# Six y pairs in the key sweep instead of four, and 35 instead of 32 steps of the second MLP product as seven products

## The chip, the core and the metric

The kernel runs on one core of one Trainium2 chip. A core has five engines that work from queues of their own: TensorE (PE in the profile, with its weight loads as PEld), VectorE (DVE), ScalarE (ACT), GpSimd (POOL) and SyncE (SP, which here only issues transfers). The metric is the device time of one execution in microseconds; the median of several is compared.

## The reference

For x of 2048 tokens with 576 features, a gate mixes a linear attention block and a channel MLP of width 4608:

```python
x = A_x
g = _sigmoid((x * gate_w).sum(-1, keepdims=True))
# a: 32 heads of 18; phi(t) = where(t > 0, t + 1, exp(t)) + 1e-6
pq, pk = phi(q), phi(k)
kv = jnp.einsum("bhsd,bhse->bhde", pk, v)
z = jnp.einsum("bhsd->bhd", pk)
o = num / den            # num = pq kv, den = pq z + 1e-6
a = o @ wo
y = _layernorm(x, axis=-1)
h = _gelu(jnp.einsum("bsd,df->bsf", y, w1) + b1)
b = jnp.einsum("bsf,fd->bsd", h, w2) + b2
return g * a + (1 - g) * b
```

## The kernel before

Every float32 operand of a large product is split into a high half, rounded to TensorE's fast float32 form (by a copy on ACT), and a low half, the rest (by a subtraction on DVE). Three products of halves replace one.

**The key sweep** goes over 16 tiles of 128 tokens, in the order `ORDER`. In each tile n TensorE projects the keys in two halves (into PSUM banks 6 and 7), adds the first part of the previous tile's products of keys and x, projects the queries in two halves (banks 6 and 7 again) and adds the rest of those products. The last three tiles leave their queries to later, so their tiles are shorter; the late queries of the first of these three follow right behind tile 15. A bank is free again when the projection in it has been through phi: Relu and Exp on ACT, then one DVE instruction that writes the keys (`k`) or the queries (`acc`). DVE and ACT also split the next tile's x, the keys (`ks`) and the tile's rows for the products (`xs`).

**Gates.** For groups of tiles (`MOMENTS`) the mean, the deviation and the gate are worked out: `gates_in` (three small DVE instructions), one step later `gates_act` (Exp, a table load, Sqrt, a table load, a dummy Exp, all on ACT), one step later `gates_out` (eight small DVE instructions) and `share_moments` (a store by POOL's queue, from which `rows` is read back over all partitions).

**Y pairs.** The normalized x, transposed, is the MLP's moving operand. It is made for two tiles at a time, a pair: the raw rows and the two tiles' x are loaded into `yr` and `rows` (both within the tile `accs`), normalized in four DVE instructions of 768 columns (`normal_pair`), combined in four DVE sums of 384 (`sum_pair`) and split in seven matrices: three double parts and a single one, each a copy on ACT and two instructions on DVE into a stage (`ys` in the profile, `y` for the last part), then stored. Part 0 needs only the normalizing, part 1 the first two sums, parts 2 and 3 the others. There are eight pairs, four for each half of the tokens.

The sweep's own work is written in order; beside it stand jobs at thirds of a tile: `run(3 * n)` behind the split of the keys, `run(3 * n + 1)` behind the queries' phi, `run(3 * n + 2)` at the tile's end. `Y_JOBS` names for each pair the third in which it is loaded, and those of its normalizing, sums and parts. The first half's four pairs are made in the sweep; the second half's four in the first half of the feed-forward part (`make_y`), one matrix at a time through `ystage`.

**The MLP** runs in 36 steps, 18 for each half of the tokens. A step's first product (up, `product`, in seven products by Strassen's scheme in Winograd's form) fills two blocks of 256 hidden features; ACT's Gelu and splits on ACT and DVE make h; the second product (down) is `one_of_seven` where the step stands in `SEVEN` (14 units of 6 matmuls of 128x288, 84 in all) and `plain_unit` where it does not (8 units of 12, 96 in all). Seven products need four sums of h, four sums of w2, seven low halves of h instead of four and four groups of w2 instead of two. `FIVES` names the steps of seven that keep one of the products in a sum of its own, with fewer evictions on DVE. `ON_DVE` tells for each sum of h, w1 and w2 whether DVE or POOL makes it. Up matmuls stream 512 columns, down matmuls 288.

The order of the feed-forward part on all engines is set by a planner, `plan`, from costs, due times and the table `TUNED`; TensorE takes the next up or the next down piece by `choose`. What the planner chose is issued in that order on each engine and stays so: every instruction is recorded through `InOrder`, so an engine never passes a waiting instruction. All instructions show the recorder's line, L120.

Of the kernel before, what the change touches and what calls it, by code (L numbers as in the profile page):

```python
# [33 lines left out]
MOMENTS = ((0, 2), (2, 4), (4, 6), (6, 8), (8, 16))  # L34
# [42 lines left out]
Y_JOBS = ((13, (16, 16, 17, 17), (18, 18, 19, 19), (18, 19, 20, 21)), (20, (22, 22, 23, 23), (25, 25, 27, 27), (25, 26, 28, 29)), (27, (31, 31, 32, 32), (33, 33, 34, 34), (34, 35, 35, 36)), (35, (37, 37, 38, 38), (39, 39, 41, 41), (40, 42, 43, 44)))  # L77
# [6 lines left out]
SEVEN = set([1, 2, 3, 4, 5, 7, 8, 9, 10, 11, 12, 14, 15, 16, 17, 18, 19, 20, 21, 22, 23, 24, 25, 26, 27, 28, 29, 30, 31, 32, 33, 34])  # L84
DVE_SUMS = set([(2, False), (2, True), (3, True), (4, False), (4, True), (6, False), (6, True)])
SEEDS = ((0, 0, 0), (0, 1, 1), (1, 0, 1))
Y_EARLY = 5000
ON_DVE = set([('h', 0, 2), ('h', 0, 6), ('h', 1, 3), ('h', 2, 2), ('h', 2, 6), ('h', 3, 4), ('h', 3, 6), ('h', 4, 2), ('h', 5, 3), ('h', 5, 6), ('h', 6, 2), ('h', 6, 3), ('h', 6, 6), ('h', 7, 2), ('h', 7, 6), ('h', 8, 4), ('h', 8, 6), ('h', 9, 4), ('h', 9, 6), ('h', 10, 2), ('h', 10, 4), ('h', 11, 2), ('h', 11, 6), ('h', 12, 4), ('h', 12, 6), ('h', 13, 4), ('h', 14, 4), ('h', 14, 6), ('h', 15, 2), ('h', 15, 4), ('h', 16, 6), ('h', 17, 3), ('h', 17, 4), ('w1', 2, 0), ('w1', 3, 0), ('w1', 10, 0), ('w1', 12, 0), ('w1', 14, 0), ('w1', 16, 0), ('w1', 17, 0), ('w2', 0, 0), ('w2', 4, 0), ('w2', 5, 0), ('w2', 8, 0), ('w2', 10, 0), ('w2', 11, 0), ('w2', 12, 0), ('w2', 14, 0), ('w2', 16, 0)])
FIVES = set([1, 2, 3, 4, 5, 7, 8, 9, 10, 11, 12, 14, 15, 16])
TUNED = (6, 7, 0, 1000, 0, {'unit': -1500, 'ytl': 1500, 'h': -1500, 'yst': 700, 'yhi': -300, 'y': -1500, 'w2': -3000, 'sum': 700, 'p': 700, 'ylo': 300, 'w1sum': -700, 'w1raw': 1500, 'evict': -1500, 'w2hi': -700, 'fin': -700, 'q2': -1500, 'seed': -3000, 'hi': -3000, 'ynorm': 3000, 'forked': -1500, 'ysum': -1500, 'q4': 6000, 'whole': 700, 'u3': -700, 'b2b': -3000, 'q1': 10000, 'out': -300, 'u1': -300, 'end': -700, 'q3': 700, 'w1st': 3000, 'attn': -700, 'fold': -300, 'w2raw': 300, 'yraw': 700}, [2, 5, 250, -500, 600, {'sum': 700, 'u3': 700, 'end': -1500, 'w2sum': -700, 'out': -3000, 'unit': -1500, 'p': -700, 'h': -300, 'evict': -700, 'hi': -1500, 'w1sum': 10000, 'seed': 3000, 'forked': 3000, 'y': 3000, 'q2': -3000, 'u1': -1500, 'q4': 6000, 'w1st': 300, 'ysum': 300, 'w2': 300, 'yraw': 1500, 'whole': 300, 'ynorm': 10000, 'attn': -3000, 'ytl': -1500, 'w1raw': -300, 'q1': 1500, 'yst': 300, 'fin': -300, 'yhi': 700, 'w2raw': 1500, 'w1': 300, 'w2hi': 6000, 'fold': 10000, 'b2b': 700}])  # L90
# [36 lines left out]
def tile_gated_mix(ctx: ExitStack, tc: tile.TileContext, x, xm, xe, wm, we, wvm, wve, wo, um, ue, w2, b1, b2, gw, out):  # L127
# [278 lines left out]
    def load_pair(sup, j):  # L406
# [3 lines left out]
        sp.dma_start(rows, moments[b][None, :, c0:c0 + 2 * P].to_broadcast([P, 2, 2 * P]))  # L410
        for a, m in enumerate((B11, B12)):
            i = ORDER[q + a]
# [147 lines left out]
    jobs = {n: [] for n in range(3 * NT)}  # L560
# [15 lines left out]
    for b, n in enumerate((9, 13, 22, 28)):  # L576
# [4 lines left out]

    for j, (loaded, normal, added, parts) in enumerate(Y_JOBS):
        at(loaded, load_pair, 0, j)
        for n, when in enumerate(normal):
            at(when, normal_pair, 0, j, n // 2, n % 2)
        for m, when in enumerate(added):
            at(when, sum_pair, 0, j, m)
        for part, when in enumerate(parts):
            at(when, split_pair, 0, j, part, lambda part=part: y_stages[part])
            at(when, split_tails, 0, j, part)  # L590
            at(when + 2, store_pair, 0, j, part)
# [290 lines left out]
    HEAR = {PE: 155, ACT: 33, DVE: 33, POOL: 78, DMA: 30}  # L882
# [141 lines left out]
    def sum_on(what, k, m=0):  # L1024
        own = ((what, k, m) in ON_DVE) != ((m, k < NCHUNK) in DVE_SUMS)
# [26 lines left out]
    def make_w1(k):  # L1052
# [5 lines left out]
        if k > 1:  # L1058
            dma(lambda: load_w1(k), raw_free["w1"] if k > 2 else [], [("w1raw", k)], 4400, 8, each=560)
            for n in range(4):  # L1060
                engine, eng = sum_on("w1", k)
# [33 lines left out]
    def make_w2(k):  # L1095
# [4 lines left out]
        if seven:  # L1100
            for n in range(4):
                engine, eng = sum_on("w2", k)
# [317 lines left out]
    def plan(lag, late, slop, slack, guard, ahead, second=None):  # L1420
        second = second or (lag, late, slop, slack, guard, ahead)
# [23 lines left out]
        next_up, next_down, shift = 0, 0, 0.0  # L1445
# [35 lines left out]
        def choose(e, gently):  # L1481
            if e == PE:
# [4 lines left out]
                if a and b:  # L1487
# [5 lines left out]
                    if ta is not None and tb is not None:  # L1493
                        if tb <= ta + 100:
# [22 lines left out]
        while any(pending.values()):  # L1517
# [6 lines left out]
            e, t = o.engine, s + o.tail  # L1524
# [92 lines left out]
```

## Time and profile before

| | |
|---|---|
| median of 3 runs | 1096.38 us (1096.2 to 1096.6) |
| span of the profiled execution, first to last instruction | 1094.1 us |
| the runs' median over this span | 2.3 us |
| sweep of the keys, first tile with its full rhythm to the key sums | 26 to 181 us |
| a tile with queries, a tile without | 11.2 us, 7.5 us |
| linear attention | to 272.6 us |
| feed-forward part, up and down matmuls | 272.6 to 1090.5 us |

The profile is of one execution. Its views are read in this manner: the page gives busy time of each engine over the whole; the view by stretches gives the same for chosen windows; the timeline lists instructions with start, length and, in brackets, the idle time before them and what ended it. A matmul's end is modelled, and they overlap, so the spacing is read from start to start.

### The profile page before, as it was taken

To read this page: it belongs to the slowest core of one execution; us is meant where nothing else is said; L and a number is where in the kernel's file an instruction comes from. 1 tells how busy PE (TensorE), PEld (TensorE's weight loads), DVE (VectorE), ACT (ScalarE), POOL (GpSimd) and SP (SyncE) were. 2 spreads that over 40 slices of the span, in tenths; PEclk is the share of its full clock that TensorE was granted. 3 is DMA by queue.
4 is the path that set the end of the run, shared out by engine and by line. 5 is a ranking of instruction groups with operands and counts; after the bars stand their busy time and mean duration, and the time that the engine had idled before them with its cause. 6 is when DMAs were issued, how large, how long until landed. Compare 5 with 4: busy or idle time off the path is not lost.

```text
span 1094.1 us, 18599 instructions
## 1 busy us (share of the span) xinstructions
PE 1087.8 (99%) x6694; PEld 996.8 (91%) x6694; DVE 917.2 (84%) x1553; ACT 687.5 (63%) x1230; POOL 235.6 (22%) x232
## 2 busy tenths in 40 slices
PE   9999999999999999999999999999999999999998
PEld 9999999999898889988889999989899999999898
DVE  4568784895799999899999997988887888878888
ACT  6677765454667887777877876455545555455552
POOL 2111112531123232332111202121122211221110
PEclk9999999999999999999999999999999999999999
DMA  6466772745745565764556559574444435444432
GB/s 186 128 88 190 171 218 102 286 173 188 252 152 195 184 206 192 235 215 161 199 174 222 195 192 395 174 253 119 138 145 118 130 119 150 132 119 119 135 100 87
DMA packets 109006, 189.72 MB, mean 173 GB/s; under 512 B 8940, under 2 KB 68604, under 8 KB 104818
## 3 DMA queue, kind: packets, MB, share of 16 engines
q1 hardware_dynamic: 108002, 187.78, 53.3%
q8 instruction: 53, 0.87, 0.3%
q10 hardware_dynamic: 720, 0.74, 0.2%
q14 instruction: 39, 0.32, 0.1%
q0 software_dynamic: 192, 0.01, 0.1%
HBM read 121.70 MB, written 66.80 MB: 172 GB/s over the span
## 4 chain that ended last, share of the span: by engine, by line
PE 93%; DVE 3%; DMA 1%; ACT 1%; issue 0%; SPq 0%; ACTq 0%; DVEq 0%
PE ps L120 93%; DVE accs L120 1%; DMA s<-in_wm 0%; DVE h L120 0%; DMA fresh<-in_ue 0%; DMA ystage<-late_acc 0%; ACT u L120 0%; DMA s<-in_we 0%; DVE wp L120 0%; DVE region L120 0%; SPq L120 0%; DVE den L120 0%; DVE fresh L120 0%; DVE ystage L120 0%; DVE u L120 0%
## 5 line engine op out<-in xcount | busy, mean ns | idle before, releaser
L120 PEld LDWEIGHTS ps<-region,h 128*128 128x128 f32 x3072 | 437.8, 188 | 30.1 <-ACT ps L120 4.3
L120 PE MATMUL ps<-region,h 128*128 128x288 f32 x3072 | 457.1, 296 | 1.0 <-DVE region L120 0.4
L120 DVE TENSOR_TENSOR accs<-ps,accs 128x576 f32<-128x576 f32 x330 | 246.1, 753 | 60.9 <-PE ps L120 54.1
L120 PE MATMUL ps<-y,wa 128*128 128x512 f32 x1008 | 257.6, 393 | 0.0
L120 PEld LDWEIGHTS ps<-y,wa 128*128 128x128 f32 x1008 | 180.9, 188 | 30.3 <-ACT ps L120 0.2
L120 POOL TENSOR_TENSOR fresh<-fresh 128x288 f32<-128x288 f32 (+1 forms) x128 | 116.4, 913 | 410.5 <-DMA fresh<-in_w 129.6
L120 PE MATMUL ps<-y,wb 128*128 128x512 f32 x756 | 199.3, 394 | 0.1
L120 DVE TENSOR_TENSOR h<-u,h 128x512 fp32r<-128x512 f32 x240 | 165.9, 704 | 8.7 <-ACT u L120 8.7
L120 PEld LDWEIGHTS ps<-y,wb 128*128 128x128 f32 x756 | 133.9, 188 | 20.9 <-ACT u L120 0.5
L120 ACT ACTIVATE region<-fresh 128x576 fp32r<-128x576 f32 (+1 forms) x132 | 81.3, 625 | 73.5 <-PE ps L120 72.9
L120 PE MATMUL ps<-y 128*128 128x288 f32 (+1 forms) x896 | 125.8, 297 | 0.3 <-DVE y L120 0.2
L120 PEld LDWEIGHTS ps<-y 128*128 128x128 f32 x896 | 122.6, 189 | 1.8 <-DVE y L120 0.4
L120 ACT ACTIVATE ps<-ps 128x576 f32<-128x576 f32 (+1 forms) x127 | 78.7, 621 | 45.0 <-PE ps L120 21.5
L120 POOL TENSOR_TENSOR u<-u 128x512 f32<-128x512 f32 x44 | 57.0, 1296 | 193.5 <-DVE h L120 54.9
L120 DVE TENSOR_TENSOR region<-fresh,region 128x576 fp32r<-128x576 f32 (+1 forms) x132 | 93.8, 723 | 1.1 <-ACT region L120 1.1
L120 ACT ACTIVATE u<-ps 128x512 f32<-128x512 f32 x73 | 43.0, 589 | 68.4 <-PE ps L120 68.2
L120 ACT ACTIVATE h<-u 128x512 fp32r<-128x512 f32 x128 | 73.5, 622 | 10.0 <-DVE u L120 5.5
L120 ACT ACTIVATE h<-u,b1s 128x512 fp32r<-128x512 f32 x73 | 52.6, 722 | 42.6 <-DVE u L120 42.4
L120 PE MATMUL ps<-wp,qt 128*128 128x288 f32 x448 | 63.0, 297 | 0.0
L120 DVE TENSOR_TENSOR u<-ps,u 128x512 f32<-128x512 f32 x74 | 50.4, 683 | 13.5 <-PE ps L120 12.7
L120 PEld LDWEIGHTS ps<-wp,qt 128*128 128x128 f32 x448 | 59.8, 188 | 0.0
L120 DVE TENSOR_TENSOR u<-u 128x512 f32<-128x512 f32 x84 | 58.1, 691 | 1.7 <-POOL u L120 1.1
(137 smaller groups left out, 1052.1 us busy)
## 6 DMA issues: line engine op xcount, KB each, us to landing
w1d<-wa SPq DMA_DIRECT2D x17, 1280.0 KB
wa<-w1d SPq DMA_DIRECT2D x68, 320.0 KB
fresh<-in_w SPq DMA_DIRECT2D x70, 288.0 KB
y<-yd SPq DMA_DIRECT2D x14, 1280.0 KB
w1d<-wb SPq DMA_DIRECT2D x17, 960.0 KB
wb<-w1d SPq DMA_DIRECT2D x51, 320.0 KB
yd<-ystage SPq DMA_DIRECT2D x28, 320.0 KB
fresh<-in_um SPq DMA_DIRECT2D x64, 128.0 KB
```

What stands on the lines that cost most here:

```text
L120: self.last = self.tc.keep_in_program_order(op(*args, **kwargs))
```

## The change

Six pairs are made in the sweep: the first half's four and two of the second half's, one every six thirds of a tile (first parts at 18, 24, 30, 36, 42 and 47). The sixth pair's last parts and their stores stand behind the late queries' projection (48) and behind the last tile's squares (49, 50), for which the list of jobs is three longer. The gates of these tiles are needed earlier, so `MOMENTS` has two more groups of two tiles; their jobs start at `GATES_AT`. `load_pair` is cut in two, and the rows are loaded six thirds after the gates' start at the earliest. `make_y` makes the last two pairs only.

Steps 0, 6 and 13 are added to `SEVEN`; `FIVES` gains 6 and 13 and loses 16. `ON_DVE` now names every sum that DVE makes, for w1 and w2 one by one. The planner gets longer hearing times, a measured cost for each matmul of a run of one kind, and a rule that stays with up matmuls until a run has `hold` of them while the down side is less than `wait` behind; `TUNED` has new numbers.

```diff
-MOMENTS = ((0, 2), (2, 4), (4, 6), (6, 8), (8, 16))
+MOMENTS = ((0, 2), (2, 4), (4, 6), (6, 8), (8, 10), (10, 12), (12, 16))
-Y_JOBS = ((13, (16, 16, 17, 17), (18, 18, 19, 19), (18, 19, 20, 21)), (20, (22, 22, 23, 23), (25, 25, 27, 27), (25, 26, 28, 29)), (27, (31, 31, 32, 32), (33, 33, 34, 34), (34, 35, 35, 36)), (35, (37, 37, 38, 38), (39, 39, 41, 41), (40, 42, 43, 44)))
+Y_JOBS = ((13, (16, 16, 17, 17), (18, 18, 19, 19), (18, 19, 20, 21)), (19, (22, 22, 23, 23), (24, 24, 25, 25), (24, 25, 26, 27)), (25, (28, 28, 29, 29), (30, 30, 31, 31), (30, 31, 32, 33)), (31, (34, 34, 35, 35), (36, 36, 37, 37), (36, 37, 38, 39)), (37, (40, 40, 41, 41), (42, 42, 43, 43), (42, 43, 44, 45)), (43, (45, 45, 46, 46), (47, 47, 48, 48), (47, 48, 48, 49)))
+GATES_AT = (9, 13, 19, 25, 31, 37)
-SEVEN = set([1, 2, 3, 4, 5, 7, 8, 9, 10, 11, 12, 14, 15, 16, 17, 18, 19, 20, 21, 22, 23, 24, 25, 26, 27, 28, 29, 30, 31, 32, 33, 34])
+SEVEN = set([0, 1, 2, 3, 4, 5, 6, 7, 8, 9, 10, 11, 12, 13, 14, 15, 16, 17, 18, 19, 20, 21, 22, 23, 24, 25, 26, 27, 28, 29, 30, 31, 32, 33, 34])
-    for b, n in enumerate((9, 13, 22, 28)):
+    for b, n in enumerate(GATES_AT):
...
+    for pair, (loaded, *_) in enumerate(Y_JOBS):
+        at(max(loaded, GATES_AT[pair] + 6), load_rows, *divmod(pair, TPB))
+        at(loaded, load_xs, *divmod(pair, TPB))
...
     projected(late[0], QUERY)
+    run(3 * NT)
     queries_out(late[0])
     moments_of(end)
+    run(3 * NT + 1)
     for part in range(2):
         add_products(end, part)
+    run(3 * NT + 2)
...
-        for j in range(TPB):
+        for j in range(len(Y_JOBS) - TPB, TPB):
...
-                        if tb <= ta + 100:
+                        if tb <= ta + 100 and not (run[0] == "up" and run[1] < hold and behind < wait and ta <= free[PE]):
```

What stands on ACT from the queries' phi of tile 12 to the keys' phi of tile 13, before (`e` is phi's Relu and Exp; `ys` are double parts of a y pair):

```order
L120 ACTIVATE xs<-xn 128x576
L120 ACTIVATE e<-ps 128x288
L120 ACTIVATE e<-e 128x288
L120 ACTIVATE e<-ps 128x288
L120 ACTIVATE e<-e 128x288
L120 ACTIVATE ys_560<-accs 128x2x384
L120 ACTIVATE ys_561<-accs 128x2x384
L120 ACTIVATE ys_562<-accs 128x2x384
L120 ACTIVATE e<-ps 128x288
L120 ACTIVATE e<-e 128x288
```

And in the change, from the second half of the queries on:

```order
L121 ACTIVATE e<-ps 128x288
L121 ACTIVATE e<-e 128x288
L121 ACTIVATE ys_565<-accs 128x2x384
L121 ACTIVATE g<-g 128x2
L121 ACT_TABLE_LOAD
L121 ACTIVATE mr_115<-mt 128x2
L121 ACT_TABLE_LOAD
L121 ACTIVATE tiny<-ones 128x1
L121 ACTIVATE ys_566<-accs 128x2x384
L121 ACTIVATE e<-ps 128x288
L121 ACTIVATE e<-e 128x288
```

The first part has moved ahead of the queries, and a gate job stands between the second and the third. Tiles 6, 8 and 10 have the same order in the change.

On DVE, from the keys of tile 15 to the copies of the sums out of PSUM, before (`y<-accs` is the last part of a pair; `acc` are the late queries, for which bank 6 and 7 wait):

```order
L120 SCALAR_TENSOR_TENSOR k<-ps,e 128x288 x2
L120 SCALAR_TENSOR_TENSOR ks<-k,ks 128x576
L120 TENSOR_TENSOR xs<-xn,xs 128x512
L120 TENSOR_TENSOR xs<-xn,xs 128x64
L120 SCALAR_TENSOR_TENSOR acc_102<-ps,e 128x288 x2
L120 COPY accs<-ps 128x512
```

And in the change, behind the same split of tile 15's rows:

```order
L121 TENSOR_TENSOR xs<-xn,xs 128x64
L121 TENSOR_TENSOR y<-accs,y 128x256
L121 SCALAR_TENSOR_TENSOR y<-y,low_rows,accs 128x128
L121 TENSOR_TENSOR accs<-accs 128x768 x4
L121 TENSOR_TENSOR accs<-accs 128x384 x2
L121 TENSOR_TENSOR ys_564<-accs,ys_564 128x2x256
L121 SCALAR_TENSOR_TENSOR ys_564<-ys_564,low_rows,accs 128x2x128
L121 TENSOR_TENSOR accs<-accs 128x384 x2
L121 TENSOR_TENSOR ys_565<-accs,ys_565 128x2x256
```

Behind these come the rest of parts 1 and 2, then the late queries. The fifth pair's last part and the whole sixth pair but its last part have come to stand ahead of them.

On TensorE the feed-forward part has 3036 down matmuls instead of 3072, and 282 runs of up matmuls between down matmuls instead of 298; the up matmuls are 1764 in both.

More of the change, by code (lines that the diff above doesn't have):

```diff
@@ L1024, in sum_on @@
     def sum_on(what, k, m=0):
[L1025 removed]
+        own = (what, k, m) in ON_DVE
         return (DVE, dve) if own else (POOL, pool)
@@ L1418, in tile_gated_mix, with plan @@
     assert len(in_order) == len(ops)
-    def plan(lag, late, slop, slack, guard, ahead, second=None):
-        second = second or (lag, late, slop, slack, guard, ahead)
+    def plan(lag, late, slop, slack, guard, ahead, second, hold, wait):
         slot, due = {o: n for n, o in enumerate(ups)}, {}
@@ L1530, in plan @@
                         late, slop, slack, guard = second[1:5]
+                        hold, wait = second[6:8]
                 else:
```

55 lines of the change are left out of this document (34 added, 21 removed).

## The prediction

> **What bounds the kernel now.** First the page: busy shares, then the chain that ended last.
>
> ```profile
> PE 1087.8 (99%) x6694; PEld 996.8 (91%) x6694; DVE 917.2 (84%) x1553; ACT 687.5 (63%) x1230; POOL 235.6 (22%) x232
> PE 93%; DVE 3%; DMA 1%; ACT 1%; issue 0%; SPq 0%; ACTq 0%; DVEq 0%
> ```
>
> TensorE sets the time: 1087.8 of 1094.1 us busy, 93% of the chain. A matmul that goes is worth its full spacing, and a wait put in front of a matmul costs its full length. So I ask of every stage how near the second engine, VectorE (DVE), stands to TensorE. The view by stretches tells: seven tiles of the key sweep with queries, the three without and what follows them, the first half of the feed-forward part, the second.
>
> ```profile
> 70.80:149.20 78.40, 78.40 (x527) 75.33 (x526) 63.08 (x137) 56.97 (x128) 12.36 (x10) 1.00 0.67 162
> 149.20:181.90 32.70, 32.70 (x204) 30.52 (x203) 22.78 (x42) 19.48 (x47) 4.30 (x3) 1.00 0.56 203
> 272.60:690.00 417.40, 416.61 (x2443) 373.29 (x2442) 388.84 (x644) 314.37 (x520) 99.69 (x95) 1.00 0.60 211
> 690.00:1090.50 400.50, 400.16 (x2396) 363.05 (x2395) 338.92 (x511) 207.88 (x342) 74.77 (x79) 1.00 0.45 135
> ```
>
> The columns are TensorE, its weight loads, DVE, ScalarE (ACT), GpSimd. In the sweep TensorE has no hole and DVE idles 15.3 of 78.4 and 9.9 of 32.7 us. In the feed-forward part TensorE is idle 0.8 and 0.3 us; DVE idles 28.6 us of the first half.
>
> **Part 1: products removed.** Steps 0, 6 and 13 have 84 matmuls instead of 96 each: 36 fewer of 128x288, all on the bounding engine. Their spacing, and what a change of stream costs:
>
> ```profile
> 279.03 4.92 PE L120 MATMUL ps<-y,wb 128*128 128x512 f32 x21
> 283.79 6.51 PE L120 MATMUL ps<-y,wa 128*128 128x512 f32 x28
> ...
> 560.15 1.78 PE L120 MATMUL ps<-y,wa 128*128 128x512 f32 x7
> 561.77 1.75 PE L120 MATMUL ps<-region,h 128*128 128x288 f32 x12
> 563.36 0.86 PE L120 MATMUL ps<-y,wa 128*128 128x512 f32 x3
> ```
>
> From 561.77 to 563.36 twelve take 1.59 us, 132.5 ns each: 36 x 132.5 = **-4.8 us**. In a long run an up matmul takes (283.79 - 279.03)/21 = 227 ns, in a run of seven (561.77 - 560.15)/7 = 231: some 30 ns a run. The change has 282 runs instead of 298: 16 x 30 ns = **-0.5 us**.
>
> What pays for it on DVE in the first half: by the order 13 more evictions, 9 more low halves of h, 6 more of w2 and 10 more sums, 38 operations; 16 on y rows and 28 on y stages have left, 44. At the stretch's mean of 388.84/644 = 0.60 us that is about 4 us less, and since evictions and low halves are the longer ones, I read it as even. TensorE's half is 5 us shorter, so DVE's idle time falls from 28.6 to some 23 us of 412. DVE still keeps up on the mean, so I take nothing for it. Waits could grow or shrink with the new sequence: at best the 1.1 us seen go, with holes too short for this view; at worst the 4.8 us are given back. The second half keeps its products; 15 more DVE operations at its mean of 0.66 are 10 us at most and find 61 us of idle time: nothing. ACT and GpSimd are far from full in both halves, and the two more small stores of gate values on POOL stand in its idle time: no cost. The loads that change places on SP come more than a tile before their use, but for the last pair's (below).
>
> **Part 2: the sweep with queries (tiles 6 to 12).** Each pair now takes two tiles, 22.4 us of TensorE, and each has its gate job in between: Exp, table load, Sqrt, table load, Exp. The trace shows such a job once beside y parts, in tile 9:
>
> ```profile
> 116.17 0.83 ACT L120 ACTIVATE ys<-accs 128x768 fp32r<-128x768 f32 x1
> 117.00 0.20 ACT L120 ACTIVATE g<-g 128x2 f32<-128x2 f32 x1
> ...
> 120.11 0.51 ACT L120 ACTIVATE y<-accs 128x384 fp32r<-128x384 f32 x1
> 120.53 0.39 ACT L120 ACTIVATE e<-ps 128x288 f32<-128x288 f32 x1
> ```
>
> ```profile
> 121.51 0.46 DVE L120 SCALAR_TENSOR_TENSOR k<-ps,e 128x288 f32<-128x288 f32 x1 [0.16 <-ACT e L120]
> ```
>
> ```profile
> 122.61 3.88 PE L120 MATMUL ps<-y 128*128 128x288 f32 x28
> ```
>
> The job holds ACT 3.11 us, the next keys' eviction ends at 121.97 and the queries' product that needs its bank starts at 122.61: 0.64 us to spare. In the change, part 2 of a pair (0.84 us on ACT, 1.0 on DVE) stands behind every such job and ahead of that eviction, and the job's inputs stand on DVE behind two sums and part 0. The spacings on DVE, from one row's start to the next:
>
> ```profile
> 150.38 3.81 DVE L120 TENSOR_TENSOR accs<-accs 128x768 f32<-128x768 f32 x4
> ...
> 159.00 1.14 DVE L120 TENSOR_TENSOR accs<-accs 128x384 f32<-128x384 f32 x2
> 160.06 0.68 DVE L120 TENSOR_TENSOR ys<-accs,ys 128x512 fp32r<-128x512 f32 x1
> ...
> 161.06 1.14 DVE L120 TENSOR_TENSOR accs<-accs 128x384 f32<-128x384 f32 x2
> ...
> 168.65 0.41 DVE L120 TENSOR_TENSOR y<-accs,y 128x256 fp32r<-128x256 f32 x1
> ...
> 169.25 0.45 DVE L120 SCALAR_TENSOR_TENSOR k<-ps,e 128x288 f32<-128x288 f32 x1
> 170.66 0.46 DVE L120 SCALAR_TENSOR_TENSOR k<-ps,e 128x288 f32<-128x288 f32 x1 [0.96 <-ACT nmean L120]
> 172.07 1.23 DVE L120 SCALAR_TENSOR_TENSOR ks<-k,ks 128x576 fp32r<-128x576 f32 x1 [0.96 <-ACT ks L120]
> 173.22 0.81 DVE L120 TENSOR_TENSOR xs<-xn,xs 128x512 fp32r<-128x512 f32 x2
> ...
> 178.00 0.46 DVE L120 SCALAR_TENSOR_TENSOR acc<-ps,e 128x288 f32<-128x288 f32 x1 [1.40 <-ACT e L120]
> 178.37 1.34 DVE L120 COPY accs<-ps 128x512 f32<-128x512 f32 x3
> ```
>
> Normalizing 0.94 each (four end after 3.81), sums 0.53 each, a double part 1.0, a single one 0.60, the 0.96 wait for ACT's half of the keys, then 1.15 and 0.73. With two key evictions (0.84) and the next x (0.95) a tile's own work is 4.6 us. Even tile: 4.6 + 4 sums 2.1 + 3 parts 3.0 + two query evictions 0.8 + gate inputs 0.3 = 10.8. Odd tile: 4.6 + gate outputs 1.3 + last part 0.6 + evictions 0.8 + normalizing 3.7 = 11.0. And a wait: from the gate's inputs to part 2, ACT takes 3.1 + 0.8, while DVE has two sums and part 1, 2.1: 1.9 us idle in order. Together 23.7 us in 22.4: **1.3 us lost per pair**, once slack is used. Walked through the queue, each of the first three pairs costs TensorE about 0.4 us at the odd tile's queries and 0.9 at the next tile's keys (their bank waits for the query eviction behind gate outputs and last part): **+4.1 us**. The bounds are 0 and twice that.
>
> **Part 3: tiles 13 to 15 and the late queries.** Here a tile lasts 7.5 us of TensorE, and two whole pairs stand on DVE where one stood. From pair 4's first normalizing, in DVE's order: 3.7; tile 14: 4.6 + sums 2.1 + parts 3.0; tile 15 (no next x): 3.7 + last part 0.6 + normalizing 3.7 + sums 2.1 + parts 3.0; then the late queries' eviction 0.8. Together 27.3 us. In the old trace that place in tile 13 comes at 159.0 plus gate outputs and last part, 160.9; so the eviction would end at 188.2 at the earliest. Who waits:
>
> ```profile
> 180.61 1.13 PE L120 MATMUL ps<-pks,ones 128*128 128x288 f32 x4
> ```
>
> The sums of the keys use the banks that this eviction frees, at 180.61 now. 188.2 + 0.1 - 180.6 = 7.7 us is the **floor**. But tile 13 starts 4.1 us later and DVE comes to it late by the fourth pair's gate, 1.8 us; TensorE is then stopped by x of tile 15 (2.2), by keys of tile 15 (1.3), and by the eviction, a hole of about 6 us. With 0.4 for the copies behind: 4.1 + 1.8 + 27.3 + 160.9 = 194.1, less 180.6, and 0.4: **+13.9 us for parts 2 and 3**. The last pair's x can be asked for only when part 1 of pair 4 has been read; its six loads land about when DVE arrives, 0 to 1 us more, which I put at nothing.
>
> **Part 4: the clock after the hole.** TensorE starts slowly and ends slowly:
>
> ```profile
> 1.13 5.49 PE L120 MATMUL ps<-ones 128*128 128x128 f32 x24 [1.13 <-DVE ones L120]
> ...
> 7.37 0.38 PE L120 MATMUL ps<-ones 128*128 128x128 f32 x2
> ```
>
> ```profile
> 1092.50:1094.10 1.60, 0.00 (x0) 0.00 (x0) 0.00 (x0) 0.00 (x0) 0.00 (x0) 0.53 0.00 0
> ```
>
> The first passes come every 0.22 us; after some 6 us of work two fit in 0.38 with their ends. And soon after the last product the granted clock (third number from the end) is 0.53. A hole of 6 us should do the same, and the work behind it would run at half rate for 3 to 6 us: I take 4, that is **+2.0 us**, between 0 and 3.
> The Trainium skill (page "TensorE: Matmul & The Clock Gate", section "Part 1: The HAM clock gate (the "warmup" mystery)") says that the clock halves after about one idle window of 3.4 us and returns after a busy one. The trace agrees at both ends. By its figure alone, an estimate, one window at half rate loses 1.7 us and the time is 1106.7.
>
> **Sum.** -4.8 - 0.5 + 13.9 + 2.0 = +10.6 us. The profiled execution has a span of 1094.1, the runs a median of 1096.4, 2.3 us of start and end around it that the change does not touch: **1107.0 us**.
>
> **Rivals.**
> *DVE takes it up* (faster). DVE idles 9.9 us between 149.2 and 181.9, and 11 us of work are added there. If work could fill that idle time, and the tiles before held their pace, the sweep would lose about 1.5 us: 1096.4 - 5.3 + 1.5 = 1092.6, with 1.1 us of old holes gone 1091.5. It decides the case from the point where the late eviction ends by 186, 5.3 us late. Against it: the engine works in order, and 0.96 us before each tile's keys and the wait behind the gate can't be filled. 6%.
> *Only the floor* is paid: 7.7 us, no clock loss, 1096.4 - 5.3 + 7.7 = 1098.8. It needs tiles 6 to 12 to hold. 8%.
> *The clock stays up*: 1105. 16%.
> *The first half becomes DVE's*: stretches there stand at 93% already; if the 4.8 us are given back, 1111.8. 10%.
> My forecast: 60%. That the edits do not do what they say is excluded by the order: 3036 products instead of 3072.
>
> **Range and chances.** Parts 2 to 4 reach from 7.7 to about 20, the feed-forward part from about -7 to -0.5. 1101 to 1111.5 leaves out the floor case, the faster one and the worst of the last. A measurement of this kernel can tell about 0.2%, 2.2 us, from no change. Faster: 6%. Within: 3%, between the floor and the fast case. Slower: 91%.
>
> **What would show it.** Part 1: 3036 products; the feed-forward part from its first product to its last 5 us shorter than 817.8. Part 2: holes before the queries of tiles 7, 9, 11 and the keys of tiles 8, 10, 12. Part 3: the key sums' matmul about 14 us later, behind a hole ended by the late queries' eviction on DVE, with DVE full from tile 13 on. Part 4: a granted clock under 1 in that stretch. I am wrong if TensorE stays closed from 83 to 195 us, or if the first half of the feed-forward part shows holes of several us.

## The result, and the profile after

| | before | after |
|---|---|---|
| median | 1096.29 us (4 runs, 1095.55 to 1096.6) | 1108.84 us (4 runs, 1107.67 to 1109.35) |
| ratio | | 1.0111, 95% interval 1.010 to 1.0123 |
| span of the profiled execution | 1094.1 us | 1105.9 us |
| first up matmul starts | 272.65 us | 291.43 us |
| from there to the start of the last matmul | 817.52 us | 810.58 us |

The kernel became slower by 12.55 us; 1107.0 was forecast, with 1101 to 1111.5 as range. Between the two profiled executions (+11.8 us) the sweep lost 18.78 us and the feed-forward part gained 6.94.

From the page of after: busy shares, TensorE and its clock in forty slices, and the chain that ended last.

```profile
PE 1088.3 (98%) x6658; PEld 995.2 (90%) x6658; DVE 956.1 (86%) x1616; ACT 704.4 (64%) x1249; POOL 247.7 (22%) x234
PE   9999997899999999999999999999999999999998
PEclk9999998899999999999999999999999999999999
PE 87%; DMA 4%; DVE 3%; ACT 3%; issue 1%; SPq 1%; ACTq 0%; DVEq 0%
```

Most of the loss stands in the slices 7 and 8, from 166 to 221 us; DMA, which had 1% of the chain, now has 4%. The stretches of the prediction once more, and one for the late part (columns as there: span, PE, PEld, DVE, ACT, POOL, clock, share of the DMA engines, GB/s):

```profile
70.80:149.20 78.40, 76.18 (x496) 70.90 (x496) 65.20 (x149) 56.99 (x128) 11.69 (x10) 1.00 0.78 182
149.20:181.90 32.70, 28.50 (x181) 26.32 (x179) 25.21 (x55) 20.28 (x44) 5.04 (x4) 1.00 0.82 182
181.90:205.00 23.10, 18.47 (x88) 17.04 (x89) 18.09 (x34) 12.76 (x29) 5.04 (x4) 0.71 0.67 239
291.40:708.80 417.40, 417.16 (x2442) 374.91 (x2441) 401.35 (x649) 322.47 (x527) 114.39 (x110) 1.00 0.58 198
708.80:1102.40 393.60, 393.50 (x2362) 357.12 (x2360) 344.92 (x516) 206.31 (x337) 71.40 (x65) 1.00 0.45 134
```

The first half of the feed-forward part is closed (0.24 us idle) although VectorE is busy 96% of it. In the sweep VectorE is not full: it still idles 7.5 of 32.7 us while TensorE has holes. So something makes VectorE wait. The holes of TensorE in after's timeline:

```profile
89.69 3.98 PE L121 MATMUL ps<-y 128*128 128x288 f32 x28 [0.32 <-DVE k L121]
96.22 4.01 PE L121 MATMUL ps<-y 128*128 128x288 f32 x28 [0.53 <-DVE accs L121]
119.87 4.00 PE L121 MATMUL ps<-y 128*128 128x288 f32 x28 [0.54 <-DVE acc L121]
143.51 4.00 PE L121 MATMUL ps<-y 128*128 128x288 f32 x28 [0.55 <-DVE acc L121]
...
170.97 3.98 PE L121 MATMUL ps<-y 128*128 128x288 f32 x28 [1.03 <-DVE k L121]
183.11 6.43 PE L121 MATMUL ps<-y 128*128 128x288 f32 x28 [4.37 <-DVE k L121]
196.71 2.26 PE L121 MATMUL ps<-pks,ones 128*128 128x288 f32 x4 [3.42 <-DVE acc L121]
199.47 5.21 PE L121 MATMUL ps<-y 128*128 128x288 f32 x28
204.52 5.66 PE L121 MATMUL ps<-accs,wv 128*126 128x126 f32 x50
```

The four short ones stand where the prediction put them, and tile 13 starts at 154.81 instead of 150.72 (0.19 us of that stood there already at tile 7, which starts at 83.71 instead of 83.52). The late queries wait 4.37 us and then take 6.43 us instead of 3.88; the key sums come at 196.71 instead of 180.61. The splits of the last two pairs on ScalarE and what SyncE issued meanwhile (SPq rows are issues) name the wait that was not forecast:

```profile
176.08 0.85 ACT L121 ACTIVATE ys<-accs 128x768 fp32r<-128x768 f32 x1 [1.91 <-DVE accs L121]
180.72 0.84 ACT L121 ACTIVATE ys<-accs 128x768 fp32r<-128x768 f32 x1 [3.79 <-DMA yd<-ys]
...
181.60 0.69 DVE L121 TENSOR_TENSOR ys<-accs,ys 128x512 fp32r<-128x512 f32 x1 [2.49 <-ACT ys L121]
...
163.10 2.03 SPq L121 DMA_DIRECT2D wot<-in_wo  x2
165.24 0.41 SPq L121 DMA_DIRECT2D yd<-ys  x1
...
168.01 0.34 SPq L121 DMA_DIRECT2D xn<-in_x  x1
180.12 0.32 SPq L121 DMA_DIRECT2D accs<-moments  x1
```

Part 2 of pair 4 may not overwrite its stage before the store of pair 3's part 2, issued at 165.24, has landed; that was at 180.64, 15.4 us later. VectorE idles 2.49 us behind it, ahead of the keys of tile 15. SyncE itself stands from 168.35 to 180.12, waiting for the moments of the last pair (in the view of SyncE's waits 11.7 us, the longest). Two transfers could be to blame: the load of `wot`, 1.4 MB, and the moments store of POOL, issued at 166.42.

### The profile page after: what moved, and what is told of

The parts are those of the page before. It is cut to its first block, busy times and chain, and to the rows that moved or that the text cites. A ratio compares the mean times of both kernels' runs of the same rounds, so it can differ in the third digit from the quotient of the medians.

```text
span 1105.9 us, 18646 instructions
## 1 busy us (share of the span) xinstructions
PE 1088.3 (98%) x6658; PEld 995.2 (90%) x6658; DVE 956.1 (86%) x1616; ACT 704.4 (64%) x1249; POOL 247.7 (22%) x234
## 4 chain that ended last, share of the span: by engine, by line
PE 87%; DMA 4%; DVE 3%; ACT 3%; issue 1%; SPq 1%; ACTq 0%; DVEq 0%
PE ps L121 87%; DMA yd<-ys 1%; DVE accs L121 1%; DMA yd<-ystage 1%; ACT e L121 1%; SPq L121 1%; DVE ys L121 1%; DMA t<-in_xm 1%; DMA s<-in_wm 0%; ACT ks L121 0%; ACT xn L121 0%; DVE xs L121 0%; ACT L121 0%; ACT y L121 0%; DVE y L121 0%
## 5 line engine op out<-in xcount | busy, mean ns | idle before, releaser
L121 PEld LDWEIGHTS ps<-region,h 128*128 128x128 f32 x3036 | 432.1, 188 | 26.2 <-issue 1.6
L121 PE MATMUL ps<-region,h 128*128 128x288 f32 x3036 | 448.9, 295 | 0.2 <-DVE accs L121 0.2
L121 DVE TENSOR_TENSOR accs<-ps,accs 128x576 f32<-128x576 f32 x344 | 254.3, 753 | 29.7 <-PE ps L121 23.3
L121 DVE TENSOR_TENSOR h<-u,h 128x512 fp32r<-128x512 f32 x249 | 181.1, 748 | 9.8 <-ACT u L121 9.5
L121 POOL TENSOR_TENSOR fresh<-fresh 128x288 f32<-128x288 f32 (+1 forms) x102 | 89.8, 883 | 322.4 <-DVE h L121 102.3
L121 POOL TENSOR_TENSOR u<-u 128x512 f32<-128x512 f32 x70 | 94.0, 1344 | 264.6 <-DVE u L121 85.0
L121 PE MATMUL ps<-y 128*128 128x288 f32 (+1 forms) x896 | 130.2, 303 | 9.1 <-DVE k L121 5.7
L121 ACT ACTIVATE ps<-ps 128x512 f32<-128x512 f32 (+1 forms) x135 | 83.8, 622 | 58.6 <-PE ps L121 38.1
L121 ACT ACTIVATE h<-u 128x512 fp32r<-128x512 f32 x140 | 81.3, 620 | 8.0 <-POOL u L121 4.5
L121 DVE TENSOR_TENSOR u<-u 128x512 f32<-128x512 f32 x70 | 48.2, 688 | 7.7 <-ACT u L121 7.1
```

Of the source, the lines that this page charges most:

```text
L121: self.last = self.tc.keep_in_program_order(op(*args, **kwargs))
```

## The experiments

Theory **Q**: the holes are those of VectorE's own order, with the clock behind them. Rivals: **W**, the load of `wot`; **J**, the moments stores hold up the other transfers; **C** is the price of the clock; and for the feed-forward part **P**, that it gains only since two pairs have left it. All ran beside the kernel before, whose median was 1096.1 to 1096.5. One caution for all single profiles: the same sweep does not always end at the same time. e2 has the sweep of after and ends it at 293.15 instead of 291.43; e7 has the sweep of before and ends it at 273.74 instead of 272.65. So differences of a microsecond or two between two profiles are read only where a wait in the rows shows them.

### The feed-forward part: e1, e2, e7

e1 has four pairs, and all else as changed; e2 has the six pairs, and steps 0, 6 and 13 plain; e7 has only the products of the change.

```diff
 e1: after.py with the Y_JOBS and MOMENTS of before, and
-GATES_AT = (9, 13, 19, 25, 31, 37)
+GATES_AT = (9, 13, 22, 28)
 e2: after.py with the SEVEN of before, and 6 and 13 taken out of FIVES
 e7: before.py with the SEVEN and FIVES of after.py
```

> The changed kernel with the four pairs, gate times and moment groups of before; all 35 steps of seven stay, and the second half's four pairs are made in the feed-forward part again. Theory Q (the fifth and sixth pair and the closer spacing overfill VectorE's queue in the sweep; the feed-forward part gains by itself): the first up matmul is back at 272.7 us, 18.8 earlier than in the changed kernel, the feed-forward part takes about 810.6 us as in the changed kernel, and the time is 1096.3 - 6.9 = 1089.4. Rival F (the three steps of seven need the two pairs out of VectorE's way; with four pairs to make, the first half of the feed-forward part is VectorE's): holes there give back 3 to 7 us, and the time is 1092.5 to 1096.3.

> The changed kernel with steps 0, 6 and 13 of the second product as plain steps again (six pairs kept). If the feed-forward part's gain is that of the 36 products alone (36 x 132.5 ns), it takes 810.6 + 4.8 = 815.4 us and the time is 1108.8 + 4.8 = 1113.6; the shorter stalls then come from the new plan and stay. If the stalls shrank because of the three steps too, it takes 817 to 818 us and the time is 1115.5. The sweep is as in the changed kernel under both: first up matmul at 291.4, granted clock 0.5 twice.

> The kernel before with the changed kernel's 35 steps of seven and its steps with a sum of their own; the sweep with four pairs, the sums' engines and the planner stay those of before. Theory P (VectorE has no room for the three steps in the first half of the feed-forward part unless two pairs leave it): the feed-forward part gets holes and takes 818 to 830 us instead of 817.5, and the time is 1097 to 1109. Rival (the products pay by themselves; it was the changed table of sums and the new planner numbers that made four pairs so dear): it takes 812.5 to 814 us and the time is 1091.5 to 1093.

Measured: e1 1115.15 us (ratio 1.0169, 1.0156 to 1.0182), e2 1114.91 (1.0172, 1.0159 to 1.0185), e7 1135.22 (1.0357, 1.0343 to 1.0371). The feed-forward part, from the first up matmul to the start of the last, took 834.6, 815.3 and 856.6 us. Its first half, from the first up matmul to the 883rd of the 1764, in before, after, e1 and e7:

```profile
272.65:667.21 394.56, 393.77 (x2307) 352.59 (x2305) 371.53 (x619) 300.87 (x497) 94.79 (x89) 1.00 0.59 203
```

```profile
291.43:680.12 388.69, 388.45 (x2270) 348.86 (x2269) 375.72 (x610) 306.63 (x501) 108.51 (x105) 1.00 0.56 190
```

```profile
274.11:686.88 412.77, 398.36 (x2270) 349.97 (x2269) 395.00 (x655) 311.32 (x515) 108.04 (x105) 0.99 0.56 196
```

```profile
273.74:707.92 434.18, 408.45 (x2271) 355.51 (x2269) 396.77 (x653) 309.89 (x515) 107.18 (x102) 0.97 0.54 185
```

e2 gives the products by themselves: 815.26 - 810.58 = 4.68 us for 36, of the 4.8 forecast. What is left of the gain, 817.52 - 815.26 = 2.26 us, belongs to the two pairs and the new plan. e1 and e7 bear P out: with four pairs left in it, the first half has 14.4 and 25.7 us of holes. And they show why: in both, VectorE has more to do there (395.0 and 396.8 us) than TensorE needs for the whole half in after (388.5). If VectorE could be busy 96.7% of the half, as in after (375.72 of 388.69), e1's 395.0 us would take 408.6, an estimate from these rows; e1 took 412.8. So of the 24.1 us that e1's half is longer than after's, some 20 are the amount of work and some 4 the order, which was made for two pairs.

e1's sweep ended at 274.1, not at 272.7. Some 0.8 of these 1.4 us come from a wait of VectorE for the first pair's rows, which the change asks for behind its x, two thirds later:

```profile
73.44 0.96 DVE L121 TENSOR_TENSOR accs<-accs 128x768 f32<-128x768 f32 x1 [1.49 <-DMA accs<-moments]
```

In the profile of after that wait is 0.57 us and hidden; in e1, e2, e4, e6 and e10 it opens a hole of 0.3 to 0.6 us ahead of tile 7's keys, and the tiles behind come 0.5 to 1.0 us later by it. It may be part of what separates after's median from its profiled run, the fastest of the four; no run was made for it.

### The late hole: e3, e6

e3 loads `wot` early; e6 stores only the first group's moments in the sweep, so that five pairs are normalized with other rows.

```diff
 e3:
-    at(40, load_wo)
+    at(12, load_wo)
 e6:
-        at(n + 2, share_moments, b)
+        if b == 0:
+            at(n + 2, share_moments, b)
```

> The changed kernel with the 1.4 MB load of wot issued at third 12 instead of 40. Theory T (a part of the late hole is ScalarE's 3.79 us wait in front of part 2 of pair 4, for a store that stands in the transfers behind wot): that wait goes, the late queries' eviction on VectorE ends 2.5 us earlier (194.4 instead of 196.9), and the time falls by 2.5 us to 1106.3. Theory Q (VectorE's queue alone): VectorE then waits for the last pair's rows or x instead, the eviction moves by less than 0.5 us, and the time is 1108.3 to 1108.8. Under both tiles 7 to 13 stay as they are (tile 13 starts at 154.8).

> The changed kernel with only the first group's moments stored by the POOL queue in the sweep; the rows of pairs 1 to 5 are read from that group, so five pairs are normalized with another pair's moments. Theory J (a moments store, 2 KB in pieces of 4 bytes, holds back everything else that the DMA engines have in hand for 10 to 14 us: the stage store issued at 165.24 landed at 180.64, together with the moments issued at 166.42): ScalarE's waits of 3.79 and 4.82 us for the stages go, SyncE no longer stands from 168 to 180 us, the late queries' eviction ends 2.5 us earlier or more, and the time falls by 2.5 to 4 us, to 1105 to 1106.3. Rival W (it was the load of wot): these waits keep at least half of their length, and the time falls by less than 1 us. Under both the losses up to tile 13 (4.1 us) stay, since they are VectorE's own order.

Measured: e3 1120.77 us (1.0225, 1.0212 to 1.0238), a miss for every theory; e6 1105.41 (1.0085, 1.0072 to 1.0099), 3.4 under the changed kernel. From e3: TensorE and VectorE in tile 6 and ScalarE's wait in the late part; a stretch around that wait; and the issue of the moments store there, with its size and the us to its landing:

```profile
90.47 5.41 PE L121 MATMUL ps<-y 128*128 128x288 f32 x28 [12.40 <-DVE k L121]
86.23 3.81 DVE L121 TENSOR_TENSOR accs<-accs 128x768 f32<-128x768 f32 x4 [14.18 <-DMA accs<-moments]
...
192.79 0.84 ACT L121 ACTIVATE ys<-accs 128x768 fp32r<-128x768 f32 x1 [2.49 <-DMA yd<-ys]
```

```profile
183.00:193.00 10.00, 8.10 (x49) 6.94 (x47) 8.57 (x16) 3.14 (x5) 1.43 (x1) 1.00 0.57 30
```

```profile
moments<-mr POOLq DMA_DIRECT2D x1, 2.0 KB, 13.5
```

What e3 loses stands in tile 6: `wot` was asked for at 56.12, ahead of the first pair's x and rows, and SyncE issued the rows only at 75.71 (in e1 at 68.96). They landed at 86.11, beside a moments store under way from 71.62 to 82.58, and VectorE waited 14.18 us.

In the late part, with no `wot` near, 2.49 of the 3.79 us of wait stay: W falls as the whole cause. The DMA engines are 57% busy there at 30 GB/s. By the trace's records this busy time is that of the other transfers' packets, of 2304 and 2560 bytes: they take up to 8.5 us each instead of the usual 0.09 to 0.10. What is under way beside them is the moments store, which takes 13.5 us to land 2 KB. Landings of the transfers around it, from the trace's records (us):

```
kernel  transfer                     issued   landed   beside it
after   yd<-ys   pair 3, part 2      165.24   180.64   moments 166.42 to 180.06, wot from 163.10
after   xn<-in_x                     168.01   182.12
e3      yd<-ys   pair 3, part 2      176.43   192.71   moments 179.79 to 193.28, no wot
e3      yd<-y    pair 3, part 3      180.16   193.00
e6      yd<-ys   pair 3, part 2      166.34   176.13   no moments, wot from 164.53 to 174.56
before  yd<-ys   pair 3, part 2      168.79   173.33   neither
```

In e3 neither store lands more than 0.6 us ahead of the moments; in e6 the store lands 9.8 us after its issue, behind `wot`, and early enough. From e6:

```profile
179.06 0.85 ACT L121 ACTIVATE ys<-accs 128x768 fp32r<-128x768 f32 x1 [0.62 <-DVE accs L121]
...
182.03 3.97 PE L121 MATMUL ps<-y 128*128 128x288 f32 x28 [1.82 <-DVE k L121]
...
188.99 3.14 DVE L121 TENSOR_TENSOR accs<-accs 128x768 f32<-128x768 f32 x4 [1.26 <-DMA accs<-in_xe]
196.69 2.26 PE L121 MATMUL ps<-pks,ones 128*128 128x288 f32 x4 [6.94 <-DVE acc L121]
```

The wait of 3.79 is gone, the hole before the late queries fell from 4.37 to 1.82, and only one stretch of half clock is left. What was late next is the last pair's x: SyncE could ask for it only at 179.68, behind pair 4's last sums (ended at 179.61), and VectorE waits 1.26 us. So the late eviction ends at 196.90 all the same (196.94 in after), with tiles that came 1.6 us later (tile 13 at 156.37).

The two profiles therefore differ by only 0.3 us in span; e6's is its slowest run, after's its fastest, and the 3.4 us are a difference of medians. From the start of tile 13 to the first up matmul e6 takes 134.8 us, after 136.6, and e3, without `wot` but with the store, 134.9. Taking away either neighbour gains 1.7 to 1.8 us there. J holds for the wait, with `wot` as a smaller part of it; the rest of the late loss stays, as Q has it.

### The clock: e5, e10

```diff
 late, end = ORDER[NT - LATE:], ORDER[-1]
+fill(40)                                  # e10: 18
 projected(late[0], QUERY)
...
+fill(30)                                  # e10: 22
 pz = [ps[:, 6 + half, :HALF] for half in range(2)]
...
+def fill(n):
+    for _ in range(n):
+        pe.matmul(ps[:, 1, KC:], ones, ones[:, :64], start=False, stop=False, skip_group_check=True)
```

> The changed kernel with 40 small ones products ahead of the late queries and 30 ahead of the key sums, into PSUM columns that nothing reads; they are short enough to end inside the two late holes (4.4 and 3.4 us). Theory C (the granted clock falls because TensorE stands idle for most of a window of 3.4 us): the granted clock stays at 1.0 there, the late queries take 3.9 us instead of 6.4 and the key sums and the next projection 1.1 and 4.0 instead of 2.3 and 5.2; only the second stretch is worth time, since VectorE sets the key sums anyway: 2.3 to 2.6 us, to 1106.3. Rival (the clock falls for another reason than idle time): it falls again at the same places and the time stays within 1 us of 1108.8.

> The changed kernel with 18 small ones products ahead of the late queries and 22 ahead of the key sums; in the run with 40 and 30 each took 0.226 us, so these take 4.1 and 5.0 and end inside the holes. Theory C: the granted clock stays at 1.0, the key sums start when VectorE has evicted (about 197) and take 1.13 us, the next projection 3.97, and the time is 2.3 to 2.6 us under the changed kernel's 1108.8: 1106.2 to 1106.5. Rival (what the clock costs is hidden behind VectorE anyway): less than 1 us.

Measured: e5 1110.28 us (1.0129, 1.0116 to 1.0143), e10 1108.89 (1.0107, 1.0094 to 1.012). Neither gains over the changed kernel. After's two stretches of half clock first, then two rows and a stretch of e5, then e10's late part:

```profile
181.80:188.60 6.80, 5.49 (x23) 5.49 (x24) 5.59 (x11) 3.77 (x11) 1.41 (x1) 0.50 0.88 276
195.50:202.20 6.70, 5.49 (x19) 4.84 (x20) 4.75 (x12) 4.40 (x11) 0.83 (x1) 0.50 0.68 259
```

```profile
178.47 9.04 PE L121 MATMUL ps<-ones 128*128 128x64 f32 x80
187.32 3.95 PE L121 MATMUL ps<-y 128*128 128x288 f32 x28
```

```profile
178.40:206.70 28.30, 28.30 (x226) 27.59 (x225) 18.94 (x36) 13.74 (x30) 3.44 (x3) 1.00 0.66 219
```

```profile
183.61 0.84 ACT L121 ACTIVATE ys<-accs 128x768 fp32r<-128x768 f32 x1 [5.58 <-DMA yd<-ys]
...
186.00 6.44 PE L121 MATMUL ps<-y 128*128 128x288 f32 x28 [2.20 <-DVE k L121]
...
200.87 1.19 PE L121 MATMUL ps<-pks,ones 128*128 128x288 f32 x4
...
202.25 3.97 PE L121 MATMUL ps<-y 128*128 128x288 f32 x28
206.06 5.66 PE L121 MATMUL ps<-accs,wv 128*126 128x126 f32 x50
```

With TensorE kept busy throughout (e5) the clock stays at 1.00, so it was the idle time (C). But in e5 the fill was too long: a small product takes 9.04 / 40 = 0.226 us, so it blocked the late queries. In e10 the first fill left a hole of 2.20 us, the clock fell, and the late queries took 6.44 us again; the second fill left none. There, from the key sums to the kv product, the time is 206.06 - 200.87 = 5.19 us; in after 204.52 - 196.71 = 7.81: the second stretch costs **2.6 us**. The first, at the late queries, is hidden, since the key sums waited for VectorE in any case. Against it, in this profile, stand 1.8 us more of the store's wait (5.58 us here, 3.79 in after's), 1.0 us of fill behind VectorE's eviction, which ended at 199.83, and 1.1 us by which the tiles came later (tile 15's keys at 172.07 instead of 170.97). The saving is read from these rows; no median shows it.

### The pairs' places: e4, e8, e9, e12

```diff
 e4: after.py without the sixth pair
-MOMENTS = ((0, 2), (2, 4), (4, 6), (6, 8), (8, 10), (10, 12), (12, 16))
+MOMENTS = ((0, 2), (2, 4), (4, 6), (6, 8), (8, 10), (10, 16))
 e9: five pairs at other thirds; MOMENTS as in e4; SEVEN without 0; ON_DVE and TUNED chosen anew
+Y_JOBS = ((13, (16, 16, 16, 16), (17, 17, 19, 20), (18, 19, 22, 22)), (20, (22, 22, 22, 24), (24, 24, 25, 26), (25, 25, 28, 28)), (26, (29, 29, 30, 30), (30, 31, 31, 31), (32, 32, 34, 34)), (32, (34, 35, 36, 37), (37, 37, 37, 37), (37, 37, 39, 41)), (37, (42, 42, 43, 43), (44, 44, 44, 49), (45, 46, 49, 49)))
+GATES_AT = (9, 12, 19, 25, 30)
-        at(max(loaded, GATES_AT[pair] + 6), load_rows, *divmod(pair, TPB))
+        at(max(loaded, GATES_AT[pair] + 4), load_rows, *divmod(pair, TPB))
 e12: e9 with load_xs ahead of load_rows from the second pair on, and
-GATES_AT = (9, 12, 19, 25, 30)
+GATES_AT = (9, 13, 19, 25, 30)
```

> The changed kernel without the sixth pair in the sweep (three pairs left to the feed-forward part). Theory Q: the spacing of six thirds costs 4.1 us up to tile 13 whatever stands behind, and the long hole is the sixth pair's: tile 13 starts at 154.8, the late part adds 0.4 us or less, the first up matmul comes at 277.1, the granted clock stays at 1.0, the feed-forward part takes 810.6 to 812, and the time is 1096.3 + 4.4 - 6.9 = 1093.8 (to 1095.3). Rival T (the store wait behind wot makes the late hole): the wait of ScalarE for pair 4's stage stays and costs 2 to 3 us more in the sweep, 1096 to 1098. Rival of equal shares (each pair the half of 18.8 us): sweep +9.4, 1098.8.

> The changed kernel with the same six pairs, their work and their gate jobs at other thirds of the sweep: normalizing from thirds 16, 21, 27, 31, 37 and 43, the sums and parts put where VectorE idles, the gates of the last pairs earlier. Theory Q (order on VectorE and ScalarE, not the amount of work, makes most of the loss): the same walk through the queues that gave +13.9 gives some 9.6 us less for the sweep (the first up matmul at 282 instead of 291.4) and the clock falls once or not at all, so 1096.5 to 1099.5. Rival (the amount: two pairs more are 11 us of VectorE's work each and the sweep is simply full): the loss only moves to other tiles, the first up matmul stays at 288 or later, and the time is above 1105.

> Five pairs in the sweep, put at thirds where VectorE idles (normalizing from 16, 22, 29, 34 and 42), the rows of the first pair asked for ahead of its x, 34 steps of seven (step 0 plain), the sums' engines and the planner's numbers chosen again for three pairs in the feed-forward part. Theory Q (the order, not the amount, for five pairs): the walk through the queues gives 0.9 us of loss in the sweep, the first up matmul at 273.6 us (to 274.6), the clock stays up, the feed-forward part takes 811.6 to 813, and the time is 1096.2 + 0.9 - 5.3 = 1091.8 (1091 to 1093.5). Rival (the fifth pair itself costs, as in the run with five pairs six thirds apart): the sweep loses 4 us or more, and the time is 1095 or more.

> The run with five spread pairs once more, with two things moved so that the x of a pair is not asked for while a moments store is under way: the second gate job a third later (13 instead of 12, so that its store is issued near 72 us and not at 64), and from the second pair on the x asked for ahead of the rows. Theory J (the two holes of that run, 6.5 us before the queries of tile 7 and 2.5 us before those of tile 13, with the half clock behind each, are x transfers held back by the moments stores issued at 64.45 and 143.30): both holes go, the loads of pair 0 land by 74 us, the first up matmul comes at 273.6 to 276 instead of 289.3, the granted clock stays at 1.0, and the time is 1091.5 to 1094. Rival (five pairs overfill VectorE's queue after all, and the holes only move): first up matmul at 280 or later, 1098 or more.

e8, 1144.46 us, tells nothing: in three of its pairs the next x was asked for ahead of the last sum or the last two, so these worked on the next pair's x and waited for it. Whether six pairs could be placed better is open.

e4: 1105.74 us (1.0091, 1.0076 to 1.0106), 12 over the forecast. The feed-forward part takes 822.2 instead of 810.6 to 812, for want of the sixth pair's leaving (P again). The sweep ends at 283.34 instead of the 277.1 expected. The profiled execution was its slowest run; its part 2 of pair 4 waits 2.70 us for a stage, and the late queries have a hole:

```profile
182.23 5.51 PE L121 MATMUL ps<-y 128*128 128x288 f32 x28 [3.31 <-DVE k L121]
```

e9: 1104.92 us (1.0071, 1.0056 to 1.0085) against 1091.8 expected. The feed-forward part took 811.3, as expected; the sweep lost 16.7. Behind tile 13 it loses nothing: from that tile's start (166.75) to the first up matmul (289.33) are 122.6 us, 121.9 in the kernel before, though a whole pair is made there, and before only the sums and parts of one. The loss is two holes ahead of it, before the queries of tiles 6 and 12, and VectorE's waits:

```profile
85.86 6.74 PE L121 MATMUL ps<-y 128*128 128x288 f32 x28 [6.53 <-DVE k L121]
159.39 5.50 PE L121 MATMUL ps<-y 128*128 128x288 f32 x28 [2.47 <-DVE k L121]
79.86 1.95 DVE L121 TENSOR_TENSOR accs<-accs 128x768 f32<-128x768 f32 x2 [6.61 <-DMA accs<-in_xe]
157.01 1.95 DVE L121 TENSOR_TENSOR accs<-accs 128x768 f32<-128x768 f32 x2 [2.62 <-DMA accs<-in_xe]
```

Both x transfers ran beside a moments store (issued at 64.45 and 143.30). e12 moves the store away from the first: 1100.11 us (1.0031, 1.0019 to 1.0042) against 1091.5 to 1094 expected. The first hole is gone. The second (the expectation calls the two tiles 7 and 13) stayed, since the store came at 133.49 and the x at 133.83; the wait ended with the pair's rows, 0.65 us behind the x. The first up matmul came at 284.12 instead of 273.6 to 276:

```profile
152.82 6.36 PE L121 MATMUL ps<-y 128*128 128x288 f32 x28 [5.71 <-DVE k L121]
150.44 1.95 DVE L121 TENSOR_TENSOR accs<-accs 128x768 f32<-128x768 f32 x2 [3.57 <-DMA accs<-moments]
```

```
kernel  x of the first pair   issued 1st to last   landed            moments store beside it
e9      six loads             64.23 to 67.39       76.74 to 82.17    64.45 to 78.95
e12     six loads             64.18 to 67.34       70.42 to 74.84    none (next 72.58)
e12     pair 3, six loads     133.83 to 137.05     145.94 to 149.77  133.49 to 145.77
```

From the last issue to the last landing the same six loads take 7.5 us without a store beside them and 14.8 with one. So most of what e9 and e12 lose stands where a moments store falls beside an x, not in VectorE's order. That five pairs would cost the sweep nothing without such a meeting is argued, not shown: no run has them without it.

### A version that beats both: e11

```diff
 e11: e1 with SEVEN without 0, the rows at GATES_AT[pair] + 4, and ON_DVE and TUNED chosen anew
```

> The sweep of the kernel before (four pairs), 34 steps of seven, the sums' engines and the planner's numbers chosen again for four pairs in the feed-forward part. If the products can be had without taking a pair out of that part, once its order is made for it: the first up matmul at 272.7, the feed-forward part 814.7 to 816, and the time is 1093.5 to 1094.8. Rival P (VectorE's work in the first half bounds it as long as four pairs are made there): 817.5 us or more, as with the changed kernel's own numbers, and 1096.3 or more.

Measured: e11 **1094.56 us**, ratio to before 0.9985 (0.9976 to 0.9993), a gain of 0.15% whose interval excludes no change, and 14 us under the changed kernel. The sweep ends at 273.5, and the feed-forward part takes 814.97, of 814.7 expected at best. The page's busy line, and the first half as above:

```profile
PE 1084.7 (99%) x6670; PEld 992.8 (91%) x6670; DVE 936.7 (86%) x1601; ACT 693.3 (63%) x1238; POOL 230.8 (21%) x220
```

```profile
273.54:666.47 392.93, 391.51 (x2282) 349.92 (x2281) 381.98 (x641) 307.31 (x508) 102.21 (x98) 1.00 0.59 204
```

VectorE is 97% busy in that half with only 1.4 us of holes. It has 13.0 us less to do there than in e1 (641 instructions instead of 655), with step 0 plain and the sums dealt out anew, and so its work fits into TensorE's time. Two of the three steps pay 2.55 us with all four pairs left where they were. That is half of the products' gain without its price: for two steps P falls. Whether the third can be had too with four pairs, no run tried; e1's 395.0 us of VectorE's work speak against it.

## Why the prediction was right

The mechanism and the sum held; three terms were mis-sized, and they lie on both sides. The late sweep cost 2.9 us more than forecast and the feed-forward part gained 1.7 more; that these partly cancel is luck.

| term | forecast | measured | from |
|---|---|---|---|
| 36 products | -4.8 | -4.7 | e2 |
| rest of the feed-forward part | -0.5 | -2.3 | before and e2 |
| tiles 7 to 12 | +4.1 | +4.1 | tile 13's start |
| tile 13 to first up matmul, with the clock | +11.8 | +14.7 | 18.78 - 4.09 |
| sum, by spans | +10.6 | +11.8 | |

**Products.** Right to 0.1 us. The mean of VectorE did not bind, as taken: its work in the first half went from 371.5 to 375.7 us, near the "even" of the prediction. e1 shows what this rested on, the two pairs' leaving: with them VectorE has 395.0 us to do in a half for which TensorE needs 388.5.

**Rest of the feed-forward part.** Only the runs were counted. The lost starts, spacings over their usual length, fell from 4.2 to 1.4 us as well; "the 1.1 us seen go, with holes too short for this view" stood as the best case and is what happened.

**Tiles 7 to 12.** Four of the six places show a hole of over 0.3 us, and the loss is 4.09. Missed: "The loads that change places on SP come more than a tile before their use". By the edit the first pair's rows are asked for at third 15 and used at third 16, a third of a tile: VectorE waited 0.6 to 1.6 us for them in after, e1, e2, e4, e5, e6 and e10.

**Late sweep.** "with DVE full from tile 13 on" is the step that failed. The walk had each part's split start when its input was there; it left out that a stage must first be stored, and gave transfers no delay. With it failed a term put at nothing, "the two more small stores of gate values on POOL stand in its idle time: no cost": the one issued at 166.42 cost POOL nothing, but the stage's store beside it landed only at 180.64. The late eviction ended at 196.94, not 194.1: 2.8 us, of which the wait shows 2.49 on VectorE. The key sums' hole was 3.4 rather than 6 us because much of it went to the late queries' hole, 4.4 us where 1.3 were forecast, and to their half clock. That the last pair's x costs nothing held in after only because the store's wait came first; e6, without that wait, has 1.26 us of it and the same end.

**Clock.** Forecast 2.0, paid 2.6 at the second stretch. There were two stretches of 6.8 us at half rate; the first cost nothing. By the Trainium skill (page "TensorE: Matmul & The Clock Gate", section "Part 1: The HAM clock gate (the "warmup" mystery)") one busy window of 3.4 us brings the clock back. By that figure the loss would be 1.7 us, an estimate. In e4 the trace agrees, with one stretch of 3.4 us behind its late hole; in after each stretch is two such windows, and the measurement decides.

**Rivals.** Only the floor, or VectorE taking it up: excluded by the holes. The clock staying up: excluded by the 0.50 rows, and e10 prices it. The first half becoming VectorE's did not come in the change, and came in e1, e4 and e7.

## What to carry to other kernels

A second engine's idle time is not room for work: walk its queue in order, with the buffers' stores and loads as waits of their own, and ask of each buffer when its last store lands. A store can be small in bytes and not small for its neighbours, as the moments store here; keep such a store away from any load or store with a deadline, and look for it where the DMA engines are busy and move little. When work is moved off an engine and other work put on it, count its work in that stage against the bounding engine's time before blaming the order.

## What the runs showed of the hardware

A moments store moves 2 KB, by the kernel's access pattern as elements of 4 bytes, and took 8.9 to 14.5 us from issue to landing in these runs. While one is under way, other packets of 2304 bytes that usually take 0.09 us take up to 8.5 us (e3, from 182 us on), and loads that land 7.5 us after the last issue take 14.8 (e12, e9). The Trainium skill (page "DMA: Bandwidth & Descriptors", section "Issuing engines are not separate DMA queues") says that transfers of all issuing engines run on the same 16 DMA engines and interleave. The delays of the neighbours fit the sharing; that the transfers interleave without such delays is not seen here. Whether the 4-byte pieces or the queue of POOL is the cause was not separated by a run. The record points to the pieces. The last group's moments, which every kernel here stores as whole rows and by SyncE, are 4 KB in after and landed 1.2 us after their issue (252.55 to 253.75). And POOL's queue brought 2.2 KB in a plain load in 4.2 us at the kernel's start. No run stored the other groups' moments as rows.

In after the granted clock is 0.50 for two stretches of about 6.8 us each, in e4 for one of 3.4 behind the late hole. In e10 it fell again though the hole before the late queries was only 2.20 us, between the fill and the product; with no hole (e5) it did not fall. Behind the second fill it stayed up.
